# Reordering the first GEMM half, splitting a pair of PSUM banks into two tiles, and spreading the last stores

## The chip, the cores and the metric

The kernel runs on one core of a Trainium2 chip. The metric is the device time of one execution in microseconds (us). The engines are PE (TensorE), DVE (VectorE), ACT (ScalarE), POOL (GpSimd) and SP (SyncE), which here only issues DMAs. Each engine runs its own instructions in the order in which they were written to its queue.

## The reference, cut to what matters

Eight batches of 576 tokens go through Nystrom attention (8 heads of 64, 32 landmarks) and two feed-forward stages. The weights `w_in` and `w_out` are 64-bit floats, all else is 32-bit.

```python
q_lm = q.reshape(B, H, 32, 18, D).mean(axis=3); k_lm = ...   # landmarks: means of 18 rows
A, Bm, C = sm(q, k_lm), sm(q_lm, k_lm), sm(q_lm, k)          # three softmaxes
for _ in range(6): Z = 2 * Z - Z @ Bm @ Z                    # inverse of Bm by iteration
x = A @ Z @ C @ v                                            # B*S x 512
r = np.maximum(x @ w_in, 0); x = (r * r) @ w_out             # first stage, d_ff 2048
e = argmax(x @ w_gate)                                       # second stage: one of 8 experts per token
out = gate * sigmoid(x @ w_output_gate)[e] * (relu(x @ w1[e]) @ w2[e])
```

## The kernel before, in words

**Stages.** The prologue computes batch 0's attention and begins to convert the weights. Then `gemm(b)` runs the first feed-forward stage for one batch after the other, in two halves of tokens (`c`, 288 columns each) and 16 tiles of the hidden dimension (`f`); "tile" below means one such step. At last `experts` runs the second stage, for each batch with the expert most of its tokens chose; tokens with another expert would be done in a loop at the end (`others`). The attention of batch b+1 is cut into steps (`unit`), which are issued between the matmuls of `gemm(b)`.

**A tile.** Six matmuls of `hp` (the hidden tile, one PSUM bank in `self.hps`), then ACT makes `r` (relu), `gh` (r squared, rounded), and `g`, r squared in full: on DVE in the first half of batch 0 (line 1273), on ACT in all others (line 1275). DVE makes `gl = g - gh` (line 1276). Two tiles later `second` multiplies `gh` and `gl` with the tile's rows of `w_out` into four accumulators (12 matmuls). Products are made of high and low parts, each in a fast 32-bit form.

**The first half's other work.** In the first half of batch 0 the weights are still being converted from 64 bits (`convert`). For each piece of 128 x 512 a 512 KB transfer brings `raw`; one cast on POOL or ACT makes `m`, one on ACT makes `r` (`r<-raw`), and DVE joins them to a `w` or `wf` (`bits`). `convert_on(f)` issues `CONV` = 2 such steps behind each tile's relu. `split_out` turns each tile's `w` into `hi` (ACT) and `lo` (DVE). `first_g_of` (tiles 1, 4, 7) folds batch 0's values into `w_in` (`chunk`, the matmuls into `two` or banks; `split_g`). `SUMS_AT` places the sums of batch 1's queries, which DVE reduces for batches 0 and 1 and POOL for the others.

**What sets the order.** The program issues instructions in the order of this text, but a scheduler in the tile framework orders each engine's queue by a simulated timeline and by priority; `high_priority(URGENT)` marks the tile's products. `follow(a, b)` makes a stand behind b in that order without a semaphore: an instruction of another engine does not wait for it on the chip. `point()` stands behind each tile's relu and three times in each `second`; it adds `self.rate` to a sum, and for each whole unit issues one step of the side work. `RATES` gives the rate for a batch and half, and until tile `B1_FROM` the sum is held down. `behind(mm)` makes a tile's first product stand behind the side step of `PACE` = 20 steps ago. `hold`, `release` and `held` put off stores and loads while weights are converted. When the conversion ends (half 1, tile 0), `swap` opens new pools and loads.

**Batch 1's steps** (`unit`): six transposes of keys, with the second sums of queries in the fourth; landmarks of keys, landmarks of queries (`bank<-ident,sums` on PE), scores C, softmax B, values, seven steps of the inverse (`dg`, `eu`, `wz` on DVE between products on PE), the transpose of `wz` that gives the weights for `chunk`, and the softmax of A. From batch 2 on keys and queries are flipped by DVE transposes instead (`flipped`, lines 576 and 580), with POOL copies.

**Tiles of a pair of banks.** `products`, `chunk` and the experts' fifth accumulator take `self.pair`, one tile of two PSUM banks:

```python
two = self.pair.tile([128, 2, 512], F32, tag="p", name="two")
banks = [two[:, 0], two[:, 1]]
```

**The last stores.** The last batch's five output tiles are stored in 18 DMAs of 64 KB by a table, `("ssss", "pppp", "sspp", "aaas", "ss")`, one letter a store: s for SP, p for POOL, a for ACT. The fifth tile is made first, then the others; ACT evacuates the second and fourth, DVE the first and third.

Of the kernel before, what the change touches and what calls it, by code (L numbers as in the profile page):

```python
# [23 lines left out]
LM = 32  # L24
# [17 lines left out]


CONV = 2.0
SUMS_AT = {7: ("q", 0)}
OUT_AHEAD = 3
FIRST_G = (1, 4, 7)
B1_FROM = 3

URGENT = 2000  # L50
G_FIRST = 2

RATES = {(0, 0): 0.3, (0, 1): 0.8}
RATE = 0.4

PACE = 20
# [13 lines left out]
STEP = 1  # L70
# [51 lines left out]
class Kernel:  # L122
    def __init__(self, tc, ins, out):
        self.tc, self.nc, self.out = tc, Lanes(self, tc.nc), out
        self.lanes, self.strict, self.due_conv, self.loaded, self.late_loads, self.at_half, self.last_hp = {}, None, 0.0, 0, 0, (0, 0), None
        self.q, self.k, self.v, self.w_in, self.w_out, self.w_gate, self.w_og, self.w1, self.w2 = ins
        self.conv, self.last_pe, self.last_h, self.marks = None, None, None, []
        self.lead = False
        self.large, self.fence, self.fenced = [], None, 0
        self.now, self.later, self.side, self.rate, self.due = 0, [], iter(()), 0.0, 0.0  # L130
        self.gt, self.at, self.made, self.g_done, self.last_gb = {}, {}, {}, 0, None
        self.held, self.whole, self.raws, self.pacer, self.ahead, self.early = [], {}, {}, None, None, None
        self.wf, self.wo, self.qk, self.vt, self.wts, self.wis = {}, {}, {}, {}, {}, {}
# [49 lines left out]
    def convert(self, jobs):  # L183
# [29 lines left out]
        def scale(i):  # L213

            raw, m = st[i], tops[i % CONV_BUFS]
            r = pool.tile([128, W], I32, tag="cr", name="r", bufs=CONV_BUFS)
            top = m.bitcast(F16).rearrange("p (n t) -> p n t", t=2)[:, :, 1]
            high = raw.bitcast(BF16).rearrange("p (n t) -> p n t", t=4)[:, :, 2]
            ops = []
            low = raw.rearrange("p (n t) -> p n t", t=2)[:, :, 0].bitcast(U32)  # L220
            if self.last_h is None and i > 4 and i % 2:
                ops.append(nc.scalar.activation(out=top, in_=high, func=ACTF.Copy))
            else:
                ops.append(nc.gpsimd.tensor_copy(out=top, in_=high))
            if self.last_h is None:
                ops.append(nc.scalar.activation(out=r, in_=low, func=ACTF.Copy, scale=2.0 ** -13))
            else:
                ops.append(nc.scalar.activation(out=r, in_=low, func=ACTF.Copy, scale=0.5, bias=2.0 ** 11))
                wide.add(i)
            if self.last_h is not None:  # L230
                for op in ops:
                    self.follow(op, self.last_h)
            st[i] = m, r

        def bits(i):
# [249 lines left out]
    def bank(self):  # L485
        b = self.banks.pop(0)
        self.banks.append(b)
        return b.tile([128, 512], F32, tag="b", name="bank")

    def load_next(self, pool=None):  # L490

        if self.conv is not None and self.loaded >= 8:
            self.late_loads += 1
            return
        self.loaded += 1
        key = next(self.order, None)
        if key is None:
            return
        nm, b, hg = key
        t = self.qk[key] = (pool or self.ld).tile([128, SEG, D], F32, tag="qk", name="t", bufs=1 if pool else 3)  # L500
        src = (self.k if nm == "k" else self.q)[b, 4 * hg:4 * hg + 4]
        self.paced(self.nc.sync.dma_start(
            out=t.rearrange("p s d -> p (s d)"), in_=src.rearrange("h (l s) d -> (h l) (s d)", s=SEG)
        ))
# [16 lines left out]
    def sums(self, u, nm, hg):  # L521

        if nm + "s" not in u:
            u[nm + "s"] = self.sm.tile([128, 2, 2, D], F32, tag=f"{nm}s", name="sums", bufs=1)
        s, t = u[nm + "s"][:, hg], self.qk[nm, u["b"], hg]
        if not u["pe"]:
            t = t.rearrange("p s d -> p (s d)")
            x = self.sm.tile([128, SEG // 2 * D], F32, tag="st", name="st", bufs=1)
# [39 lines left out]
    def flipped(self, u, nm, hg):  # L568
# [4 lines left out]
        def put(to, p, i):  # L573
            src = t[p, :, LM * i:LM * i + LM]
            if nm == "k":
                self.nc.vector.transpose(  # L576
                    out=to.rearrange("p (r i l) -> p i r l", r=R6, l=LM), in_=src.rearrange("p (i r) d -> p i r d", r=R6)
                )
            else:
                self.nc.vector.transpose(out=to.rearrange("p (s l) -> p s l", l=LM), in_=src)  # L580


        for i in range(2):
# [43 lines left out]
    def products(self, u, nm, lm, i):  # L627

        if u["early"] and i:
            banks = [self.bank() for _ in range(2)]  # L630
        else:
            two = self.pair.tile([128, 2, 512], F32, tag="p", name="two")
            banks = [two[:, 0], two[:, 1]]
        with self.run_of():
            for half in (1, 0):
                for j in range(4):
# [172 lines left out]
    def values(self, u, hg):  # L809
# [15 lines left out]
        )  # L825
        if (b, 1) not in self.vt:
            self.load_v(b, 1)
        elif hg == 1:
            self.hold(lambda: self.load_v(b + 1, 0))

    def inverse(self, u, i):

# [131 lines left out]
    def unit(self, u):  # L964

        both = [(hg, i) for hg in range(2) for i in range(3)]
        if u["pe"]:
            for hg, i in both:
                self.transposed(u, "k", hg, i)
                if (hg, i) == (1, 0):  # L970
                    self.sums(u, "q", 1)
                yield STEP
        else:
            for hg in range(2):
# [9 lines left out]

        self.landmarks(u, "k")
        yield STEP
        self.landmarks(u, "q")
        yield STEP

# [51 lines left out]
    def prologue(self, right):  # L1041
# [66 lines left out]
        next(pw, None)  # L1108
        cv(2)
        self.release(2)  # L1110
        self.load_next()
        self.values(u, 0)
        for _ in range(3):
            next(a0)
# [24 lines left out]
    def chunk(self, b, n, rows):  # L1139

        if b == 0 and n == 0:
            banks = [self.bank() for _ in range(2)]
        else:
            two = self.pair.tile([128, 2, 512], F32, tag="p", name="two")
            banks = [two[:, 0], two[:, 1]]
        with self.run_of():
            for g in (1, 0):
                for j in (3, 2, 1, 0):
# [72 lines left out]
    def convert_on(self, f):  # L1221

        self.due_conv += CONV
        while self.due_conv >= 1.0:
            self.due_conv -= 1.0
            next(self.conv, None)
        self.release(1)
        if f in SUMS_AT:
            self.sums(self.ahead, *SUMS_AT[f])

# [5 lines left out]
    def gemm(self, b, swap=None, last=None):  # L1236

        nc = self.nc
        for c in range(2):
# [6 lines left out]
            for f in range(NFC):  # L1246
# [20 lines left out]
                gh = self.g3.tile([128, HC], F32R, tag="gh", name="gh", bufs=3)  # L1267
                gl = self.g3.tile([128, HC], F32R, tag="gl", name="gl", bufs=3)
                with self.tc.high_priority(URGENT):
                    nc.scalar.activation(out=r, in_=hp[:, 0:HC], func=ACTF.Relu)  # L1270
                    nc.scalar.activation(out=gh, in_=r, func=ACTF.Square)  # L1271
                    if (b, c) == (0, 0):
                        nc.vector.tensor_tensor(out=g2, in0=r, in1=r, op=ALU.mult)
                    else:
                        nc.scalar.activation(out=g2, in_=r, func=ACTF.Square)  # L1275
# [9 lines left out]
                if c == 1 and f == 0 and self.conv is not None:  # L1285
# [4 lines left out]
                    self.release(len(self.held))  # L1290
                    for _ in range(self.late_loads):
                        self.load_next()
                    swap()
                if c == 0 and f == 8:
                    self.load_at(b, 1)
                if last is not None and c == 1 and f in (5, 8, 11, 13):
                    next(last)
# [136 lines left out]
    def jobs(self):  # L1434
# [3 lines left out]
        def job(b):  # L1438
            def store(t, y):
# [3 lines left out]
                    return  # L1443

                q = dict(s=nc.sync, a=nc.scalar, p=nc.gpsimd)
                for i, e in enumerate(("ssss", "pppp", "sspp", "aaas", "ss")[t][:rows_of(t) // LM]):
                    q[e].dma_start(out=rows[4 * t + i], in_=y[LM * i:LM * i + LM])

            return dict(
# [8 lines left out]
    def experts(self, jobs):  # L1458
# [66 lines left out]
        def second(i, h, acc):  # L1525
# [2 lines left out]
            first, last = f == 0, f == NF2 - 1  # L1528
            if first:
                acc.extend(self.acc.tile([128, DM], F32, tag="b", name="y") for _ in range(4))  # L1530
                acc.append(self.pair.tile([128, 2, 512], F32, tag="p", name="y")[:, 0])
            ends = []

            def in_turn(mm, begin, end):
# [236 lines left out]
```

## Time and profile before

| | |
|---|---|
| runs | 1245.49, 1246.2, 1247.0 us; median 1246.2 |
| profiled execution | 1246.25 us; span from first to last instruction 1244.2 us |
| busy share of the span | PE 97%, ACT 49%, DVE 49%, POOL 31% |
| mean granted TensorE clock | 0.984 |
| PE's busy tenths in 40 slices | 6889899899999999999999999999999999999996 |
| DVE's | 7893755766556555655646532234332323323231 |
| granted clock in the slices | 8699999999999999999999999999999999999999 |
| DMA engines' | 9963043152232142142042210153434435443231 |

A slice is 31.1 us; a digit is the busy share in tenths (9 is 90% or more; the clock's are tenths of full speed). The prologue takes the first slice, the first half of batch 0 ends at about 101 us, its second half at about 157; the GEMMs take until about 800 us, the experts the rest.

### The profile page before, as it was taken

The page shows a single profiled execution, that of the slowest core. Times are in us where ns is not written, and L with a number is a line of the kernel's source. Part 1 is how long each engine was busy: PE and PEld are TensorE (multiplying, and loading weights), DVE is VectorE, ACT ScalarE, POOL GpSimd, SP SyncE. Part 2 cuts the span into 40 slices and gives each one's busy share as a digit, 9 for nine tenths or more (in the row PEclk, how much of TensorE's full clock was granted, in tenths as well). Part 3 has the DMA queues.
Part 4 walks back from the last instruction along what each step waited for, and adds up shares of the span by engine and source line. Part 5 has one row for each costly group of instructions (what it writes and reads, how often), then busy time and mean ns, then how long its engine had stood idle before and what let it go on. Part 6 is the DMA issues. An engine that isn't in the chain of part 4 may idle for free.

```text
span 1244.2 us, 25082 instructions
## 1 busy us (share of the span) xinstructions
PE 1207.0 (97%) x9838; PEld 1078.3 (87%) x9838; DVE 606.4 (49%) x1512; ACT 610.0 (49%) x1413; POOL 390.0 (31%) x524
## 2 busy tenths in 40 slices
PE   6889899999999999999999999999999999999996
PEld 4679788989989989989989989998888888888885
DVE  7893755766556555655646532234332323323231
ACT  6675355555564564555565555543342433434331
POOL 6540440613332241340341100253342433424220
PEclk8699999999999999999999999999999999999999
DMA  9963043152232142142042210153434435443231
GB/s 341 365 240 107 20 160 120 31 174 77 72 142 78 66 148 77 56 158 78 25 169 59 95 63 1 40 169 87 136 115 138 139 92 160 116 130 111 82 97 40
DMA packets 88407, 142.24 MB, mean 114 GB/s; under 512 B 6430, under 2 KB 61758, under 8 KB 84702
## 3 DMA queue, kind: packets, MB, share of 16 engines
q1 hardware_dynamic: 87854, 139.97, 34.6%
q8 instruction: 79, 1.29, 0.4%
q0 software_dynamic: 288, 0.43, 0.1%
q14 instruction: 42, 0.34, 0.1%
q10 hardware_dynamic: 144, 0.20, 0.1%
HBM read 117.47 MB, written 23.11 MB: 113 GB/s over the span
## 4 chain that ended last, share of the span: by engine, by line
PE 91%; DVE 5%; DMA 1%; ACT 1%; issue 1%; POOL 0%; POOLq 0%; ACTq 0%; DVEq 0%; SPq 0%
PE hp L475 32%; PE acc L475 31%; PE y L475 17%; PE two L471 4%; PE bank L471 2%; PE bank L104 2%; PE bank L483 1%; DVE x L576 1%; PE acc L104 1%; PE pl L471 1%; DMA raw<-in_moe_w_in_dram 1%; DMA raw<-in_moe_w_out_dram 0%; PE hp L104 0%; DVE lo L104 0%; DVE ma L687 0%
## 5 line engine op out<-in xcount | busy, mean ns | idle before, releaser
L475 PE MATMUL acc<-gl,hi 128*128 128x288 f32 x964 | 273.2, 301 | 2.7 <-DVE gl L104 1.6
L475 PE MATMUL acc<-gh,lo 128*128 128x288 f32 x964 | 270.0, 297 | 0.0
L475 PE MATMUL hp<-ab,gb 128*128 128x288 f32 x1434 | 239.3, 302 | 0.1
L475 PE MATMUL y<-s,h 128*128 128x512 f32 (+1 forms) x896 | 223.3, 396 | 0.8 <-ACT h L1516 0.5
L1276 DVE TENSOR_TENSOR gl<-g,gh 128x288 fp32r<-128x288 f32 x224 | 115.0, 514 | 214.6 <-ACT g L1275 212.2
L475 PEld LDWEIGHTS hp<-xs,s 128*128 128x128 f32 x1536 | 212.4, 188 | 7.2 <-DVE ls L1727 0.3
L475 PEld LDWEIGHTS hp<-ab,gb 128*128 128x128 f32 x1434 | 202.4, 189 | 18.7 <-issue 12.7
L475 PE MATMUL hp<-xs,s 128*128 128x288 f32 x1536 | 217.0, 295 | 0.2 <-DVE ls L1727 0.2
L1270 ACT ACTIVATE r<-hp 128x288 f32<-128x288 f32 x224 | 92.0, 411 | 229.5 <-PE hp L475 228.3
L475 PE MATMUL acc<-gh,hi 128*128 128x288 f32 x964 | 198.8, 301 | 0.1
L475 PEld LDWEIGHTS y<-s,h 128*128 128x128 f32 (+1 forms) x896 | 160.7, 184 | 38.2 <-ACT h L1516 0.7
L475 PEld LDWEIGHTS acc<-gl,hi 128*128 128x128 f32 x964 | 181.9, 189 | 9.5 <-issue 2.2
L475 PEld LDWEIGHTS acc<-gh,lo 128*128 128x128 f32 x964 | 182.0, 189 | 1.4 <-issue 1.4
L280 POOL TENSOR_TENSOR s<-r,s 128x256 fp32r<-128x256 f32 x128 | 102.0, 818 | 234.0 <-ACT s L268 234.0
L475 PEld LDWEIGHTS acc<-gh,hi 128*128 128x128 f32 x964 | 149.6, 188 | 19.8 <-ACT gh L1271 14.2
L1516 ACT ACTIVATE h<-hp 128x288 fp32r<-128x288 f32 x128 | 52.5, 411 | 188.0 <-PE hp L475 172.5
L1519 DVE SCALAR_TENSOR_TENSOR h<-hp,h 128x64 fp32r<-128x64 f32 (+2 forms) x192 | 62.6, 354 | 167.0 <-ACT h L1516 166.5
L268 ACT CAST s<-r 128x512 fp32r<-128x512 f32 x128 | 77.6, 617 | 70.7 <-PE y L475 56.9
L1271 ACT ACTIVATE gh<-r 128x288 fp32r<-128x288 f32 x224 | 99.5, 444 | 6.4
L274 DVE TENSOR_TENSOR s<-r,s 128x512 fp32r<-128x512 f32 x64 | 50.6, 791 | 102.8 <-ACT s L268 102.8
L1275 ACT ACTIVATE g<-r 128x288 f32<-128x288 f32 x224 | 96.0, 428 | 0.0
L587 POOL COPY x<-x 32x576 f32<-32x576 f32 x48 | 32.9, 685 | 173.4 <-DVE x L576 106.0
(263 smaller groups left out, 1327.9 us busy)
## 6 DMA issues: line engine op xcount, KB each, us to landing
r<-in_moe_w_dram SPq DMA_DIRECT2D x128, 256.0 KB
wi<-win SPq DMA_DIRECT2D x28, 1024.0 KB
t<-in_k_dram SPq DMA_DIRECT2D x16, 576.0 KB
t<-in_q_dram SPq DMA_DIRECT2D x16, 576.0 KB
v<-in_v_dram SPq DMA_DIRECT2D x32, 288.0 KB
x_d<-x SPq DMA_DIRECT2D x16, 576.0 KB
xr<-x_d SPq DMA_DIRECT2D x16, 576.0 KB
raw<-in_moe_w_in_dram SPq DMA_DIRECT2D x16, 511.8 KB
```

The costliest lines, as they stand in the source:

```text
L104: return self.kernel.in_lane(self.name, fn(*args, **kw))
L268: hi = self.nc.scalar.copy(out=t[:, 0], in_=raw)
L274: lo_eng.tensor_tensor(out=t[:, 1], in0=raw, in1=t[:, 0].bitcast(F32), op=ALU.subtract)
L280: self.nc.gpsimd.tensor_tensor(out=out[:, p], in0=in0[:, p], in1=in1[:, p], op=op)
L471: self.in_run(lambda: self.nc.tensor.matmul(out, **kw))
L475: mm = self.nc.tensor.matmul(out, **kw)
L1270: nc.scalar.activation(out=r, in_=hp[:, 0:HC], func=ACTF.Relu)
L1271: nc.scalar.activation(out=gh, in_=r, func=ACTF.Square)
L1275: nc.scalar.activation(out=g2, in_=r, func=ACTF.Square)
L1276: nc.vector.tensor_tensor(out=gl, in0=g2, in1=gh.bitcast(F32), op=ALU.subtract)
L1516: nc.scalar.activation(out=h[:, t0:t1], in_=hp[:, 0:HC], func=ACTF.Relu)
L1519: nc.vector.scalar_tensor_tensor(out=h[:, to + a:to + z], in0=hp[:, a - t0:z - t0], scalar=0.0, in1=h[:, a:z].bitcast(F32), op0=ALU.max, o ...
```

## The change

- First half: batch 1's query sums move from tile 7 and the fourth side step to tiles 10 and 11, with a wait in the steps before the queries' landmarks; the side steps begin at tile 5 instead of 3, with a rate of 0.9 instead of 0.8 in the second half. The third load of batch 1's queries and keys (its first query tile) is issued at tile 2 instead of in the prologue, its first values after `swap` instead of held in the prologue. A conversion's second cast is ordered behind the newest relu instead of behind its product. For odd tiles g is made on ACT. The second half's operand is made at tile 13 instead of 8 (batch 0 alone).
- Batch 2's key and query flips on DVE are ordered behind the newest tile's first product.
- The pair of banks is two tiles of one bank each.
- The last stores have another table.

```diff
-SUMS_AT = {7: ("q", 0)}
+SUMS_AT = {10: ("q", 0), 11: ("q", 1)}
-B1_FROM = 3
+B1_FROM = 5
-RATES = {(0, 0): 0.3, (0, 1): 0.8}
+RATES = {(0, 0): 0.3, (0, 1): 0.9}
@@ scale, in convert
-            if self.last_h is not None:
-                for op in ops:
-                    self.follow(op, self.last_h)
+            if self.last_relu is not None:
+                for op, e in zip(ops, (self.last_h, self.last_relu)):
+                    self.follow(op, e)
+    def two(self):
+        return [self.pair.tile([128, 512], F32, tag=f"p{i}", name="two") for i in range(2)]
@@ sums
+        u[nm + "n"] = hg + 1
@@ put, in flipped
-                self.nc.vector.transpose(
+                op = self.nc.vector.transpose(
...
+            if u["b"] == PE_BATCHES:
+                self.follow(op, self.last_h)
@@ products; chunk alike
-            two = self.pair.tile([128, 2, 512], F32, tag="p", name="two")
-            banks = [two[:, 0], two[:, 1]]
+            banks = self.two()
@@ values
-        elif hg == 1:
-            self.hold(lambda: self.load_v(b + 1, 0))
+        elif hg == 1 and self.conv is None:
+            self.load_v(b + 1, 0)
@@ unit
                 self.transposed(u, "k", hg, i)
-                if (hg, i) == (1, 0):
-                    self.sums(u, "q", 1)
...
         self.landmarks(u, "k")
         yield STEP
+        while u.get("qn", 0) < 2:
+            yield STEP
         self.landmarks(u, "q")
@@ prologue
         self.release(2)
-        self.load_next()
@@ convert_on
         self.release(1)
+        if f == 2:
+            self.load_next()
@@ gemm
-                    nc.scalar.activation(out=r, in_=hp[:, 0:HC], func=ACTF.Relu)
+                    self.last_relu = nc.scalar.activation(out=r, in_=hp[:, 0:HC], func=ACTF.Relu)
...
-                    if (b, c) == (0, 0):
+                    if (b, c) == (0, 0) and f % 2 == 0:
...
                     for _ in range(self.late_loads):
                         self.load_next()
+                    self.load_v(1, 0)
                     swap()
-                if c == 0 and f == 8:
+                if c == 0 and f == (8 if b else 13):
                     self.load_at(b, 1)
@@ store, in jobs
-                for i, e in enumerate(("ssss", "pppp", "sspp", "aaas", "ss")[t][:rows_of(t) // LM]):
+                for i, e in enumerate(("spsp", "apsp", "sapp", "saps", "sa")[t][:rows_of(t) // LM]):
@@ second, in experts
-                acc.append(self.pair.tile([128, 2, 512], F32, tag="p", name="y")[:, 0])
+                acc.append(self.pair.tile([128, 512], F32, tag="p0", name="y"))
```

## Rows read from the trace of the kernel before

**Rows 1.** Stretches: length, busy us (instructions) by engine, clock, DMA share, GB/s.
```profile
36.00:48.00 12.00, 8.14 (x41) 4.55 (x34) 8.71 (x13) 7.21 (x14) 6.84 (x8) 0.50 1.04 372
62.00:76.00 14.00, 10.65 (x88) 9.30 (x86) 14.00 (x19) 10.89 (x25) 7.96 (x9) 1.00 0.81 315
76.00:101.20 25.20, 25.20 (x243) 22.98 (x228) 21.10 (x55) 16.66 (x40) 5.66 (x5) 1.00 0.44 160
132.40:157.40 25.00, 20.55 (x154) 17.76 (x146) 18.52 (x46) 8.89 (x22) 13.68 (x21) 0.93 0.00 1
157.40:200.00 42.60, 42.56 (x420) 36.46 (x420) 29.20 (x77) 25.89 (x66) 14.55 (x23) 1.00 0.40 138
200.00:1233.90 1033.90, 1031.60 (x8033) 928.71 (x8033) 465.76 (x1180) 489.48 (x1138) 304.29 (x406) 1.00 0.31 98
1233.90:1244.20 10.30, 0.00 (x0) 0.00 (x0) 0.03 (x1) 0.67 (x1) 2.55 (x6) 0.70 0.41 112
```
**Rows 2.** Waits of PE from 36 to 76: total us, times, longest.
```profile
PE acc L104 <- DVE gl L104: 2.4, 3, 1.1
PE hp L104 <- ACT r L104: 2.0, 2, 1.8
PE two L104 <- DVE wf L104: 1.5, 1, 1.5
```
**Rows 3.** Timeline of ACT: start, us, instruction, idle before it, releaser.
```profile
42.13 0.66 ACT L104 ACTIVATE r<-raw 128x512 int32<-128x512 uint32 x1 [2.79 <-DMA raw<-in_moe_w_in_dram]
...
43.73 0.40 ACT L104 ACTIVATE r<-hp 128x288 f32<-128x288 f32 x1
...
1233.88 0.69 ACT L1582 ACTIVATE yo<-y,rt 128x512 f32<-128x512 f32 x1 [0.72 <-PE y L475]
```
**Rows 4.** Timeline of PE around tile 1's product.
```profile
40.40 1.96 PE L104 MATMUL two<-wf,wt 64*32 64x512 f32 x16
44.18 1.81 PE L104 MATMUL hp<-ab,gb 128*128 128x288 f32 x6 [1.82 <-ACT r L104]
```
**Rows 5.** The chain that ended last: start, us, what.
```profile
34.40 7.63 DMA raw<-in_moe_w_in_dram
```
**Rows 6.** Timeline of SP, which issues the loads.
```profile
33.01 0.33 SPq L104 DMA_DIRECT2D t<-in_q_dram  x1
```
**Rows 7.** Groups on DVE, 0 to 160: count, busy us, mean ns, idle before.
```profile
L104 DVE TENSOR_REDUCE sums<-t 128x32 f32<-128x576 f32 x12 | 13.3, 1175 | 0.2 <-DMA t<-in_k_dram 0.2
L104 DVE TENSOR_TENSOR g<-r 128x288 f32<-128x288 f32 x16 | 7.7, 480 | 1.8 <-ACT r L104 1.8
...
L576 DVE STREAM_TRANSPOSE x<-t 32x576 f32<-32x576 f32 x4 | 3.1, 769 | 0.1
L576 DVE STREAM_TRANSPOSE x<-t 128x576 f32<-128x576 f32 x4 | 2.9, 754 | 0.0
```
**Rows 8.** Timeline of PE late in the second half.
```profile
138.05 0.40 PE L475 MATMUL acc<-gl,hi 128*128 128x288 f32 x1 [1.61 <-DVE gl L104]
```
**Rows 9.** Timeline of PE: batch 1's landmarks, its last transpose, the next product.
```profile
84.49 0.66 PE L104 MATMUL bank<-ident,sums 128*64 128x128 f32 x8
...
151.89 0.30 PE L483 MATMUL bank<-ident,wz 128*128 128x128 f32 x1 [0.43 <-DVE wz L849]
...
156.30 1.09 PE L471 MATMUL two<-wi,wt 64*32 64x512 f32 x16
```
**Rows 10.** Timeline of DVE in the second batch's GEMM.
```profile
189.61 2.76 DVE L580 STREAM_TRANSPOSE x<-t 128x576 f32<-128x576 f32 x4 [0.48 <-PE two L471]
```
**Rows 11.** The last stores by issuer: count, ns min/median/max, first and last start.
```profile
L1447 SPq DMA_DIRECT2D out_dram<-yo x9: 314/419/1532, 1232.6 to 1237.8; - x9
L1447 POOL DMA_DIRECT2D out_dram<-yo x6: 496/498/547, 1233.5 to 1236.0; - x6
L1447 ACTq DMA_DIRECT2D out_dram<-yo x3: 386/448/1883, 1234.6 to 1236.9; - x3
```
**Rows 12.** Waits of ACT over the whole span.
```profile
ACT gb L1190 <- DVE gb L1191: 16.5, 20, 1.4
```

More of the change, by code (lines that the diff above doesn't have):

```diff
@@ L124, in __init__ @@
         self.tc, self.nc, self.out = tc, Lanes(self, tc.nc), out
-        self.lanes, self.strict, self.due_conv, self.loaded, self.late_loads, self.at_half, self.last_hp = {}, None, 0.0, 0, 0, (0, 0), None
+        self.lanes, self.strict, self.due_conv, self.loaded, self.late_loads, self.at_half, self.last_hp, self.last_relu = {}, None, 0.0, 0, 0, (0, 0), None, None
         self.q, self.k, self.v, self.w_in, self.w_out, self.w_gate, self.w_og, self.w1, self.w2 = ins
@@ L579, in put @@
             else:
-                self.nc.vector.transpose(out=to.rearrange("p (s l) -> p s l", l=LM), in_=src)
+                op = self.nc.vector.transpose(out=to.rearrange("p (s l) -> p s l", l=LM), in_=src)
+            if u["b"] == PE_BATCHES:
+                self.follow(op, self.last_h)
         for i in range(2):
@@ L1143, in chunk @@
         else:
-            two = self.pair.tile([128, 2, 512], F32, tag="p", name="two")
-            banks = [two[:, 0], two[:, 1]]
+            banks = self.two()
         with self.run_of():
```

## The prediction

> **What bounds the kernel now.** The page's first and second parts (in the table above) say that TensorE is the engine to watch: 97% busy, nearly all slices at 9. So I cut the span into stages and asked for each engine's busy time in each [rows 1]; the reader looks for stages where PE's busy time falls short of the stage. From 200.0 to the last matmul at 1233.9 PE is busy 1031.6 of 1033.9 us: an edit that shortens nothing on PE can win 2.3 us there at most, over 1000 us. What is left to win lies in four places: 36 to 48 us (idle 3.9 us, at half clock), 62 to 76 us (idle 3.35), 132.4 to 157.4 us (idle 4.45, mean granted clock 0.93) and the 10.3 us after the last matmul.
>
> In the first two places the waits of PE between 36 and 76 us [rows 2] name the causes: 2.4 us for VectorE's gl, 2.0 for ScalarE's r, 1.5 for VectorE's wf, 5.9 us together (what is left of the idle time lies before tile 0's product). Two readings explain them. On ScalarE the relu of tile 0 starts at 43.73 only, though PE had gone on to other work at 40.40: ahead of it in ScalarE's order stood a conversion cast, r<-raw, that waited 2.79 us for its transfer [rows 3, 4]. PE's next product then waited 1.82 us for that relu [rows 4]. From 62 to 76 us VectorE is busy 14.0 of 14.0 us [rows 1]: everything that PE waits for stands in VectorE's queue. The third place is the same picture: PE waits 1.61 us for a gl in it [rows 8], and among VectorE's groups there the two largest are eight transposes at line 576, 3.1 + 2.9 us, which flip batch 2's keys, work that nobody needs before the next GEMM [rows 7].
>
> **The change part by part.**
>
> *Casts behind the relu (last_relu).* The two casts of tile 0's conversion steps are now ordered after tile 0's relu, so the relu can start at about 40.5 instead of 43.73. PE's 1.82 us goes; next late is gl of tile 0, which comes forward with the relu. Bounds: 0 (the cast now waits behind the relu and its conversion is later) to 2.5 us (with tile 0's share of the gl waits). Taken: 1.8. The same transfer is shortened, too: it was issued at 34.40 and landed 7.63 us later [rows 5], right behind a 576 KB load of batch 1's queries at 33.01 [rows 6], which moves to tile 2; at the 372 GB/s of that stretch [rows 1] the load is 1.6 us of transfer. The load of batch 1's values, two DMAs of 288 KB, leaves the stretch altogether. Neither is a second gain: they secure the first. Both now stand later in SP's queue; the values stand behind batch 2's key loads there, and the side step that reads them waits if they are late (in the last rival).
>
> *Queries' sums to tiles 10 and 11, and g of odd tiles on ScalarE.* Four reductions of 1.175 us, 4.7 us, leave the full stretch from 62 to 76, and with them the products g of tiles 5, 7 and 9, 3 x 0.48 = 1.4 us [rows 7]; ScalarE, busy 10.9 of 14.0 there, takes the latter. 6.1 us of VectorE's 14.0 against 3.35 us of idle PE: these waits can go whole. But the reductions come back in tiles 10 and 11. From 76 to 101.2 us VectorE is busy 21.1 of 25.2 [rows 1]: 4.1 us free, 5.5 with the odd tiles' g gone, for 4.7. The first half of that stretch is the fuller one, so I let a third of the 4.7 (1.6 us) be met by PE again. For waits of 5.9 us in all, the two edits together give 5.9 - 1.6 = 4.3 us; bounds 0 and 5.9, and below nothing if all 4.7 of the reductions stood ahead of the landmarks that PE runs next (5.9 - 4.7 still leaves 1.2, so a loss needs more than them).
>
> *Second batch's steps from tile 5, at 0.9 a point in the second half.* The steps' matmuls are the same; they move from a stretch in which PE waited to one in which it is full, for two transposes of keys, about 0.5 us, inside the margin above. The wait for both sums stops the side steps only (one step is lost, at tile 10). What it costs if the chain that follows becomes late is the last rival.
>
> *Batch 2's transposes behind the product of their own GEMM (flipped).* Eight transposes, 6.0 us, leave the 25.0 us in which VectorE is busy 18.5 [rows 1, 7]. The idle 4.45 us and the lowered clock, 25.0 x 0.07 = 1.7 us of PE's work, make 6.2 us that can go. What is late next is batch 1's own chain of inverses, PE to VectorE and back, for which I leave 2.0 us. Taken: 4.2; bounds 1.5 and 6.2. They come to the stretch from 157.4 to 200, where VectorE is busy 29.2 of 42.6. The same eight transposes of batch 2's queries already lie there, four of them in one piece at 189.61 [rows 10], and PE is idle 0.04 us in all of it [rows 1]. Taken: 0; bound 2 us.
>
> *Pair of banks as two tiles.* With one tile ScalarE's second cast waited for VectorE's read of the other bank, 16.5 us in 20 waits [rows 12]. No wait of PE hangs on them in the full stages: 0, bounds -0.5 and +0.2. `load_at` at tile 13, the second half's operand: ScalarE and GpSimd work with two tiles left to hide it: 0.
>
> *Last stores.* Before, SP issues 9 of the 18 stores, from 1232.6 to 1237.8, GpSimd 6, ScalarE 3 [rows 11]; from SP's last issue to the span's end are 6.4 us, which stay. After, SP has 7, GpSimd 7, ScalarE 4. GpSimd: 7 x 0.50 from about 1233.2 ends near 1236.7. ScalarE now issues stores between its evacuations, 0.39 to 0.45 each; two before the last evacuation, 1233.88 [rows 3], so that this starts some 0.6 us later, ends near 1235.2, and SP's last issue starts near 1236.1, or 1.1 later if the slow issue there (1.53 against 0.42) repeats. A gain of 0.6 to 1.7; taken 1.2, bounds 0.4 and 2.0.
> The Trainium skill ("DMA: Bandwidth & Descriptors", "Rules for kernel authors") speaks against such a split: stores spread over several issuers share the same DMA engines, and only issue time is saved. By it alone the gain would be the lower bound, 0.4 us; the DMA share of 0.41 after the last matmul [rows 1] says that issue is what bounds, and 1.2 stays.
>
> **The sum.** 4.3 + 4.2 + 1.2 = 9.7 us less. The profiled execution took 1246.25 us (span 1244.2 and 2.05 around it), which is the median of the runs (1246.2) within 0.1: 1246.25 - 9.7 = 1236.5 us. With all lower bounds of the gains and all bounds of loss (2 from 157.4 on, 0.2 for the pair) it is 1246.6, with all upper bounds 1231.6.
> The Trainium skill ("TensorE: Matmul & The Clock Gate", "What's actually happening") says the clock is halved after idleness and given back once PE has been kept busy. The trace agrees (0.50 from 36 to 48 us with PE idle a third of it); by the rule an earlier end of the waits would also bring full speed earlier, and the sum would be about 1 us better.
>
> **The rivals.**
> *Only the second half gains.* VectorE is the limit from 62 to 90 us by its total work: what leaves tiles 7 to 9 is met in tiles 10 and 11, where the landmarks stand on PE right behind the sums. For it: VectorE is full there, and the sums are read at once. Against: 5.5 us free for 4.7. Then 1246.25 - 4.2 - 1.2 = 1240.9.
> *Only the first half gains.* The stall from 132.4 is batch 1's chain, not batch 2's transposes. For it: its steps hang one on another through PE and VectorE, whatever else VectorE does. Against: the 6.0 of 18.5 us that VectorE is rid of. Then 1246.25 - 4.3 - 1.2 = 1240.8.
> *It doesn't do what it says.* The orders of the engines come from a simulated timeline; the hoisted casts and transposes may be replaced by others of the same length. Then about 1245.
> *Slower: batch 1's chain sets the end of the second half.* From the landmarks of its queries at 84.49 to its last transpose at 151.89 it takes 67.7 us, and the next batch's product stands at 156.30 [rows 9]. The change begins it two tiles later: a tile of the first half is (101.2 - 44.18) / 15 = 3.8 us (tile 1's product [rows 4] to the second half's start, the bound of a stretch in [rows 1]), so 7.6. If the chain keeps its length, it ends at 159.8, 3.5 us past the product, PE stands idle and the clock falls for another 1.7: 1246.25 + 5.2 - 1.2 = 1250.3. What the first half gains brings the chain's start forward by as much, so it is slower only if that gain is under about 1.5 us. For it: dependent steps, and the values' load now late in SP's queue. Against: the rate of 0.9, and that the chain was long because VectorE was full.
>
> **Chances.** The forecast 0.57, second half only 0.15, first half only 0.12, no effect 0.07, slower 0.09. The time is the forecast's, 1236.5 us (its own range 1232 to 1240). The range is 1231 to 1244.5: it takes in both half gains, and leaves out the slow rival, most of no effect and a few hundredths below. A change of under 0.2%, 2.5 us, can't be told from none here: faster 0.83, same 0.08, slower 0.09.
>
> **What would show it.** Tile 0's relu on ScalarE within 0.5 us of its product; no wait of PE for gl or wf from 60 to 76 us; no line 576 before the second GEMM; PE idle under 2.5 us and the clock at 1.00 around 130 to 155 us; SP's last store issued 0.6 to 1.7 us earlier against the last matmul. Wrong would be PE waiting for `sums` at tiles 10 to 12, or for `eu` and `wz` at the end of the second half as now, or for batch 2's transposes after 157 us.

## The result, and the profile after

The changed kernel takes 1260.64 us (median; 1260.09 to 1262.17) beside 1246.6 us of the kernel before (1245.49 to 1247.59): ratio 1.0115, 95% interval 1.0097 to 1.0132, so 14 us slower. The forecast was 1236.5 us.

The profiled execution took 1261.19 us, its span is 1259.4 us. To see where the time came, I cut both traces where the first relu of a half batch starts, so that a stretch holds the same work in both. The windows of the kernel before (columns as in [rows 1]):

```profile
102.16:161.59 59.43, 54.98 (x509) 49.72 (x511) 29.48 (x70) 26.36 (x65) 15.16 (x22) 0.97 0.21 68
161.59:306.46 144.87, 144.80 (x1421) 127.62 (x1420) 91.10 (x237) 81.45 (x206) 46.17 (x72) 1.00 0.35 113
306.46:450.19 143.73, 143.42 (x1281) 129.17 (x1282) 82.91 (x206) 78.90 (x196) 51.73 (x79) 1.00 0.30 101
450.19:815.54 365.35, 364.53 (x3258) 333.91 (x3257) 184.02 (x502) 200.90 (x503) 81.78 (x124) 1.00 0.23 76
815.54:1233.90 418.36, 417.22 (x2466) 370.44 (x2464) 134.17 (x309) 152.03 (x296) 139.16 (x155) 1.00 0.39 114
```

The same stretches of the changed kernel, ahead of them the one that answers to the first of [rows 1], behind them the one that answers to the last:

```profile
36.00:48.00 12.00, 9.49 (x62) 5.07 (x47) 11.16 (x17) 9.62 (x20) 7.79 (x9) 0.71 1.04 341
...
98.71:158.11 59.40, 56.64 (x511) 51.40 (x509) 24.77 (x64) 27.50 (x67) 10.64 (x15) 0.94 0.21 68
158.11:316.88 158.77, 155.58 (x1424) 129.79 (x1424) 97.53 (x249) 81.22 (x207) 53.89 (x84) 1.00 0.32 104
316.88:461.57 144.69, 144.69 (x1281) 129.21 (x1280) 80.65 (x201) 77.83 (x195) 49.00 (x75) 1.00 0.29 100
461.57:832.16 370.59, 369.78 (x3258) 334.91 (x3257) 182.78 (x501) 199.24 (x503) 82.30 (x124) 1.00 0.23 75
832.16:1250.46 418.30, 417.21 (x2466) 370.45 (x2464) 134.10 (x309) 152.01 (x295) 138.55 (x155) 1.00 0.38 115
1250.46:1259.40 8.94, 0.02 (x1) 0.00 (x0) 0.11 (x1) 0.69 (x1) 3.11 (x7) 0.74 0.46 129
```

Difference of the lengths, in us: the first half, up to 102.16 and 98.71, -3.45; the second half of batch 0, -0.03; batch 1 and the first half of batch 2, +13.90; the next three halves, +0.96; batch 4 to the last relu, +5.24; the expert part, -0.06; the tail, -1.36. Together +15.2, the difference of the spans. So the first half and the stores gained about what was forecast, the second half nothing, and 20 us came in places where the forecast had put 0. In batch 1 and the first half of batch 2 some of it is waiting: PE is idle 3.2 us there (158.77 less 155.58), 0.07 before, most of it for VectorE's gl (changed kernel, PE, 158 to 320):

```profile
PE acc L475 <- DVE gl L1281: 2.7, 4, 1.5
```

From batch 4 on waiting is not the cause. TensorE runs the same 3258 matmuls, was full before and is full after, yet its busy time grows by 5.25 us (364.53 to 369.78). A wait doesn't show like that. The groups of PE show it; of the kernel before (columns: engine, tiles, shape, count | busy us, mean ns of one | idle before):

```profile
PE 1207.0 (97%) x9838; PEld 1078.3 (87%) x9838; DVE 606.4 (49%) x1512; ACT 610.0 (49%) x1413; POOL 390.0 (31%) x524
L475 PE MATMUL acc<-gl,hi 128*128 128x288 f32 x964 | 273.2, 301 | 2.7 <-DVE gl L104 1.6 <-DVE gl L1276 1.1
L475 PE MATMUL hp<-ab,gb 128*128 128x288 f32 x1434 | 239.3, 302 | 0.1
L471 PE MATMUL two<-wi,wt 64*32 64x512 f32 x448 | 30.5, 601 | 0.0
L471 PE MATMUL two<-x,lm 64*32 64x288 f32 x416 | 22.6, 415 | 0.0
```

and of the changed kernel:

```profile
PE 1221.6 (97%) x9838; PEld 1079.0 (86%) x9838; DVE 604.4 (48%) x1504; ACT 608.7 (48%) x1421; POOL 387.8 (31%) x525
L475 PE MATMUL hp<-ab,gb 128*128 128x288 f32 x1434 | 242.2, 303 | 0.7 <-ACT r L104 0.5
L471 PE MATMUL two<-wi,wt 64*32 64x512 f32 x448 | 34.6, 601 | 0.0
L471 PE MATMUL two<-x,lm 64*32 64x288 f32 x416 | 31.9, 415 | 0.0
```

PE's busy time grew by 14.6 us with the same 9838 matmuls. The two groups that write `two`, the pair of banks, hold 13.4 of it (9.3 and 4.1), at an unchanged mean of one matmul, 415 and 601 ns. A mean that stays while the group's busy time grows says that fewer of them run at the same time. The timeline of PE shows it. Batch 5's product run of the kernel before (start, us, instruction), 8 matmuls in 16 records (two records of the trace for each of these matmuls):

```profile
465.92 0.68 PE L471 MATMUL two<-x,lm 64*32 64x288 f32 x4
466.52 0.40 PE L475 MATMUL acc<-gl,hi 128*128 128x288 f32 x1
...
471.50 0.26 PE L1411 MATMUL pc<-x,ones 128*32 128x40 f32 x2
471.69 0.70 PE L471 MATMUL two<-x,lm 64*32 64x288 f32 x12
472.32 0.40 PE L475 MATMUL acc<-gl,hi 128*128 128x288 f32 x1
```

The same run in the changed kernel:

```profile
476.47 0.69 PE L471 MATMUL two<-x,lm 64*32 64x288 f32 x8
477.09 0.35 PE L471 MATMUL pt<-lg,i 128*32 128x80 f32 x8
...
478.88 0.67 PE L471 MATMUL two<-x,lm 64*32 64x288 f32 x2
479.48 0.40 PE L475 MATMUL acc<-gl,hi 128*128 128x288 f32 x1
...
481.27 0.67 PE L471 MATMUL two<-x,lm 64*32 64x288 f32 x2
481.87 1.07 PE L475 MATMUL hp<-ab,gb 128*128 128x288 f32 x6
...
484.46 0.68 PE L471 MATMUL two<-x,lm 64*32 64x288 f32 x4
485.07 0.40 PE L475 MATMUL acc<-gl,hi 128*128 128x288 f32 x1
```

From its start to the start of what follows, a piece of 2 records holds PE for 0.60 us, of 4 for 0.60 or 0.61, of 8 for 0.62, of 12 for 0.63. A piece costs by being a piece, not by its length, and it also costs beside it: behind a piece the first large matmul holds PE 0.24 us and the next ones 0.13 (changed kernel, starts at 479.48, 479.72 and 479.85), and the hp group grew by 2.9 us. Counting as one piece what runs of one such group with nothing else between on PE, there are 67 pieces of `two` in the trace before and 85 after. Why the run fell apart stands on VectorE, whose transposes make the operand x (changed kernel):

```profile
477.97 0.77 DVE L584 STREAM_TRANSPOSE x<-t 32x576 f32<-32x576 f32 x1
...
479.75 0.77 DVE L584 STREAM_TRANSPOSE x<-t 32x576 f32<-32x576 f32 x1
```

They end at 478.74 and 480.52, and the two pieces of 2 records start at 478.88 and 481.27: some matmuls of a run have their operand earlier than others. The program issues a run bank by bank, four matmuls each, and two of the four have their operand late. While both banks were one tile, the matmuls behind a late one stayed behind it: 4 records went ahead, and the run was cut once. With two tiles 8 go ahead, and large matmuls get in between the others. That these 8 are the early ones of both banks is read from the code and the counts; the rows don't name the bank. The Trainium skill ("TensorEngine Tiling (Array Packing)", "Tiling Modes") says that a change of tiling mode drains TensorE; it gives no price. The trace fits that, though it doesn't show a drain by itself: a 64*32 piece between 128*128 matmuls holds PE 0.60 us however short it is.

### The profile page after: what moved, and what is told of

Read it like the earlier page. It is cut to its first block, busy times and chain, and to the rows that moved or that the text cites. A ratio compares the mean times of both kernels' runs of the same rounds, so it can differ in the third digit from the quotient of the medians.

```text
span 1259.4 us, 25031 instructions
## 1 busy us (share of the span) xinstructions
PE 1221.6 (97%) x9838; PEld 1079.0 (86%) x9838; DVE 604.4 (48%) x1504; ACT 608.7 (48%) x1421; POOL 387.8 (31%) x525
## 4 chain that ended last, share of the span: by engine, by line
PE 88%; DVE 6%; DMA 4%; ACT 1%; issue 1%; POOL 0%; SPq 0%; POOLq 0%; DVEq 0%; ACTq 0%
PE hp L475 31%; PE acc L475 30%; PE y L475 17%; PE two L471 5%; PE bank L471 3%; DMA win<-wf 1%; PE bank L483 1%; DMA v<-in_v_dram 1%; DVE x L580 1%; DMA raw<-in_moe_w_in_dram 1%; PE pl L471 1%; DMA raw<-in_moe_w_out_dram 1%; DVE w L104 0%; DVE gl L1281 0%; DVE ma L692 0%
## 5 line engine op out<-in xcount | busy, mean ns | idle before, releaser
L475 PE MATMUL hp<-ab,gb 128*128 128x288 f32 x1434 | 242.2, 303 | 0.7 <-ACT r L104 0.5
```

Source lines behind the costliest of these rows:

```text
L475: mm = self.nc.tensor.matmul(out, **kw)
```

## The experiments

Theory: the cut runs cost the time, and they come from the two tiles. Rivals: the new order of batches 0 to 2 costs it; or two tiles cost by themselves. The 14 runs below, each in five rounds beside the kernel before (1246.0 to 1246.7 us in the four groups). Pieces are those of the traces; the expectations count them in the programs as built, which lists some cuts that the trace doesn't show:

| kernel | us | ratio to before, interval | pieces |
|---|---|---|---|
| before | 1246.2 | 1 | 67 |
| changed | 1260.64 | 1.0115 (1.0097, 1.0132) | 85 |
| changed, one tile (e1) | 1244.02 | 0.9984 (0.9975, 0.9993) | 69 |
| two tiles alone (e2) | 1260.69 | 1.0113 (1.0097, 1.0128) | 86 |
| moved flips alone (e3) | 1247.00 | 1.0003 (0.9994, 1.0012) | 69 |
| stores alone (e4) | 1245.30 | 0.9990 (0.9981, 0.9999) | 67 |
| changed, runs in order (e5) | 1250.35 | 1.0034 (1.0021, 1.0048) | 78 |
| changed, one tile, flips back (e6) | 1243.13 | 0.9977 (0.9966, 0.9988) | 67 |
| whole runs alone (e8) | 1246.20 | 0.9999 (0.9990, 1.0008) | 61 |
| e6 with whole runs (e9) | 1244.45 | 0.9982 (0.9973, 0.9991) | 61 |
| changed, whole runs (e10) | 1244.28 | 0.9988 (0.9980, 0.9997) | 67 |
| casts, odd g, loads, stores (e11) | 1241.40 | 0.9964 (0.9951, 0.9977) | 71 |
| e11 and moved flips (e12) | 1241.48 | 0.9962 (0.9949, 0.9975) | 73 |
| casts alone (e13) | 1242.65 | 0.9975 (0.9966, 0.9983) | 67 |
| two tiles and whole runs (e14) | 1249.87 | 1.0028 (1.0018, 1.0038) | 67 |
| e11, two tiles, whole runs (e15) | 1241.06 | 0.9956 (0.9943, 0.9969) | 66 |

**Which part costs the time: e1 and e2.** e1 is the changed kernel with

```diff
-        return [self.pair.tile([128, 512], F32, tag=f"p{i}", name="two") for i in range(2)]
+        two = self.pair.tile([128, 2, 512], F32, tag="p", name="two")
+        return [two[:, 0], two[:, 1]]
```

and e2 the kernel before with the opposite edit.

> The changed kernel with the pair of banks back as one tile [128, 2, 512]; all else as changed. Theory (broken runs): a run of small matmuls that is cut costs a whole pass more for each piece, 0.69 + 0.68 us for two pieces against 0.72 us for the whole run of x,lm, so about 0.65 us a piece, and the traces have 67 such pieces before and 85 after. With one tile the program has 74 of them: 11 x 0.65 = 7 us, up to 11 x 0.75 = 8 us with what DVE's later results add, come back, so 1252 to 1254 us if that is all, and less (down to 1246.6: 1246.6 + 7 x 0.65 - 3.45 of the first half - 1.4 of the stores) if each cut run also holds up the engine behind it. Rival (the new order in the first two batches sets the loss, the pair is innocent): 1258 us or more.

> The kernel before with only the pair of banks as two tiles. The program has 86 pieces of small matmuls against 67 of the kernel before. Theory (broken runs): 19 x 0.65 = 12.4 us more, so 1259 us (1256 to 1261), with the busy time of TensorE 12 to 15 us up. Rival (the loss is the order of the first two batches): 1246.6 us, within 1 us.

One tile takes 16.6 us off the changed kernel, and two tiles alone make the kernel before as slow as the whole change did, as expected of e2. The rival of the new order is out; the cost of the pair is 14.5 us. e1 came out below its expectation, whose lowest bound was 1246.6: its gain is larger than the pieces alone (16 x 0.65 = 10.4). Part of the rest is the time beside a piece; how much that is worth was not tried.

**Two tiles or cut runs: e5 and e10.** e5 adds to the changed kernel, for each matmul of a run, an order behind the one before it; e10 only lets the product runs begin with the matmul whose operand comes last:

```diff
+        prev = self.last_pe                        (e5, in_run)
...
+        self.follow(self.last_pe, prev)
```

```diff
-                for j in range(4):                 (e10, products)
+                for j in (2, 3, 0, 1):
```

> The changed kernel, its pair still two tiles, with each small matmul of a run put behind the one before it on TensorE's order (no semaphore: an order only). Theory (broken runs): what costs time is the pieces, not the two tiles; the program has 74 pieces, as many as with one tile, so the time is that of the changed kernel with one tile, 1244.0 us (1243 to 1247). Rival (two banks in two tiles cost by themselves, in their waits or in where the tiles lie): 1258 to 1261 us.

> The changed kernel as it is, its pair two tiles, with the product runs begun with the matmul whose operand comes last (order 2, 3, 0, 1 of j). The program has 73 pieces of small matmuls against 85 in the changed kernel's trace; what is left broken are chunks' and products' runs of the first batches, cut between the two banks. Theory (price by the piece, 0.6 us for x,lm and 1.0 us for wi,wt): 12 x 0.6 = 7.2 us less than the changed kernel's 1260.6, 1253.4 us, and up to 3 us of it given back where the kernel before gave back 3.1 us for the same edit (its run starts later, and VectorE's softmax comes in one lump): 1253 to 1257 us. Rival (two tiles cost by themselves): 1259 us or more.

Both keep two tiles. With 78 pieces the time is 1250.35, with 67 it is 1244.28 us: most of the loss goes with the pieces, and two tiles need not cost by themselves. Neither met its expectation. e5 should have taken 1243 to 1247 us; 78 pieces are left in its trace, where e1 has 69, and the count is not all: from batch 4 on it has the 27 pieces of the kernel before and still takes 366.83 us against 365.35. Of e10 I had expected less, 1253 to 1257; it has 18 pieces less than the changed kernel, not 12 as counted ahead, and its batches from 4 on are faster than those of the kernel before. The run of above is one piece now, held 0.65 us (e10, PE; then the same stretches as above, and the two groups):

```profile
472.88 0.72 PE L471 MATMUL two<-x,lm 64*32 64x288 f32 x16
473.53 0.26 PE L1417 MATMUL pc<-x,ones 128*32 128x40 f32 x2
```

```profile
154.29:308.33 154.04, 151.70 (x1425) 129.33 (x1425) 95.50 (x248) 80.94 (x206) 52.48 (x83) 1.00 0.32 107
308.33:451.15 142.82, 142.47 (x1277) 128.70 (x1278) 80.45 (x202) 77.78 (x196) 49.81 (x77) 1.00 0.29 101
451.15:814.24 363.09, 362.56 (x3258) 333.32 (x3257) 180.76 (x501) 200.08 (x503) 82.44 (x124) 1.00 0.23 77
```

```profile
L471 PE MATMUL two<-wi,wt 64*32 64x512 f32 x448 | 34.6, 601 | 0.0
L471 PE MATMUL two<-x,lm 64*32 64x288 f32 x416 | 19.9, 415 | 0.0
```

From batch 4 on e10 takes 363.09 us, 7.5 less than the changed kernel and 2.3 less than the kernel before, with 12 pieces there against 21 and 15: 0.83 and 0.75 us a piece. What it still loses lies in batch 1 and the first half of batch 2, 154.04 against 144.87 us, where runs of wi,wt are still cut between the banks (34.6 against 30.5 us) and the moved flips lie.

**Is a piece always worth its 0.6 us: e8 and e9.** The edit of e10 alone, in the kernel before (e8) and in e6 (e9).

> The kernel before with one edit: the eight matmuls of a product run begin with the one whose operand comes last (order 2, 3, 0, 1 of j for 0, 1, 2, 3), so that the first of them waits and the other seven follow at once. The program has 61 pieces, one a run, against 67. Theory (broken runs): 6 x 0.65 us = 3.9 us less, 1242.3 us (1241.5 to 1243.5). Rival (the pieces' own time is covered, and what two tiles cost is something else): 1246.2 us, within 1 us; slower if the later start of a run delays VectorE's softmax.

> The changed kernel with one tile for the pair, the flip transposes where they were before, and the product runs begun with the matmul whose operand comes last. By the theory the sum of the two: 1241.2 us less 3.9 us = 1237.3 us (1236 to 1239). By the rivals 1241 us (only the first half) or 1244 to 1245 us (neither).

No. In e8 the group falls by 4.0 us, as it should, and the time stays, as the rival said. The same view of e8:

```profile
L475 PE MATMUL acc<-gl,hi 128*128 128x288 f32 x964 | 275.3, 303 | 4.2 <-DVE gl L1276 2.8 <-DVE gl L104 0.9
...
L471 PE MATMUL two<-x,lm 64*32 64x288 f32 x416 | 18.6, 415 | 0.0
```

PE's matmuls on gl are busy longer there than in the kernel before (273.2) and wait 4.2 us for VectorE, against 2.7. With one tile the whole run starts when the last operand comes, and VectorE then gets both banks at once; gl waits behind them. That VectorE's batch is the reason is read from these rows and was not tried by itself. From batch 4 on PE is idle 2.97 us of 367.39 in e8, against 0.82 before. e9 says the same: 1237.3 us was expected, it took 1244.45, no faster than e6 (1243.13), with 367.46 us from batch 4 on. With two tiles (e10, the same edit) the batches from 4 on kept the gain.

**The moved flips: e3, e6, e12.** e3 is the kernel before with

```diff
+            if u["b"] == PE_BATCHES:
+                self.follow(op, self.last_h)
```

> The kernel before with only the flip transposes of the third batch (index 2) put behind the last gate tile's work. The prediction's step: 4.2 us less, 1242.4 us. Theory of the trace after: the second half gains nothing, because the second batch's own softmax and inverse fill VectorE there, and the transposes cost up to 2.4 us where they lie now, so 1246.6 to 1249 us; and if the 74 pieces of small matmuls that the program has (67 before) cost 0.65 us each as well, 7 x 0.65 = 4.6 us more, 1251 us (1249 to 1254).

> The changed kernel with one tile for the pair and with the third batch's (index 2) flip transposes left where they were before. The traces so far: with the moved transposes alone the second half of batch 0 is 5.0 us shorter, and 4.5 us of it are gone by batch 4 (index), 2.0 us as idle time of TensorE behind gl and the rest as busy time; with all but the two tiles 4.5 us are won by the end of batch 0 and all are gone by batch 4. Theory (the moved transposes give the loss back): without them the first half's 3.5 to 3.9 us stay, with the stores' 1.2 us that makes 1241.2 us (1240 to 1242.5). Rival (the batches 1 to 3 end at a time that something else sets, VectorE or a load, and eat whatever was won): 1244 to 1245 us.

The windows of e3 at the same work:

```profile
103.50:157.96 54.46, 52.91 (x509) 48.07 (x510) 24.20 (x64) 26.58 (x65) 10.97 (x15) 1.00 0.23 75
157.96:207.29 49.33, 47.95 (x460) 41.47 (x461) 30.62 (x81) 28.77 (x74) 17.58 (x29) 1.00 0.37 125
207.29:306.01 98.72, 98.72 (x973) 87.72 (x972) 62.34 (x162) 52.39 (x133) 31.90 (x49) 1.00 0.31 104
306.01:451.12 145.11, 144.08 (x1273) 128.14 (x1272) 86.29 (x207) 78.63 (x195) 53.20 (x82) 1.00 0.28 100
```

The second half falls from 59.43 to 54.46 us with the clock at 1.00: 5.0 won. Then 3.2 and 1.4 us are given back (148.05 against 144.87, 145.11 against 143.73), 0.4 is left, less than the 1.3 us by which the first half of this execution was longer (103.50 against 102.16), and the run ends no faster. One wait shows in the first of these stretches, where the flips lie now (e3, PE, 157 to 210):

```profile
PE acc L475 <- DVE gl L1278: 1.3, 1, 1.3
```

Beside it two runs are cut that were whole. e6, without the flips, is no slower than e1, but doesn't reach the expected 1241.2: its second half is 62.0 us long, 2.6 more than before, with one long wait (PE, 98 to 161):

```profile
PE bank L471 <- DVE dg L947: 4.2, 1, 4.2
```

That is batch 1's own chain, which the change starts two tiles later.

**The first half: e11, e12, e13.** e11 is e6 with the queries' sums, the rate and the start of batch 1's steps put back as here, e12 the same with the moved flips, e13 the kernel before with the casts' order alone:

```diff
-SUMS_AT = {10: ("q", 0), 11: ("q", 1)}
+SUMS_AT = {7: ("q", 0)}
-B1_FROM = 5
+B1_FROM = 3
-RATES = {(0, 0): 0.3, (0, 1): 0.9}
+RATES = {(0, 0): 0.3, (0, 1): 0.8}
...
+                if (hg, i) == (1, 0):
+                    self.sums(u, "q", 1)
```

> Of the change only the casts behind the relu, the odd gates' products, the moved loads and the new stores; the pair one tile, the flip transposes, the queries' sums, the rate and the tile from which the second batch's steps start as before. Theory (the moved sums make the second half longer: with them, and without the moved flips, 2.6 us of the first half's 3.7 us are lost again there, behind dg and at half the clock): the first half gains 2.5 to 3.5 us and keeps it, with the stores' 1.2 us that makes 1242 us (1241 to 1243.5). Rival (any earlier start of the second half is lost in it, whatever is moved): 1245 us.

> The same with the flip transposes of the third batch moved as well. From the runs so far: the first half gains 2.5 to 3.5 us, the second half 5.0 us more, batches 1 to 3 give back 4.5 us, the stores 1.2 us: 1241.5 us (1240.5 to 1243). Rival (batches 1 to 3 give back all that was won by their start, as with the changed kernel with one tile, where 4.5 us were won and 4.6 given back): 1245 us.

> The kernel before with one edit: the converter's casts on ScalarE put behind the last gate tile's relu instead of its first matmul. The prediction's step: 1.8 us less, 1244.2 us, won before the first relu at 43.7 us. Rival (the cast is only later by as much, and the weights that wait for it with it): 1246.0 us, within 0.5 us.

All three forecasts of direction held. In its trace e13 reaches the second half 3.2 us earlier and the last relu 4.4 us earlier (the trace is of its fastest execution, 1240.44 us; its runs go up to 1246.01), the others 3.0 and 2.5 us earlier at the second half: nearly all of the first half's gain is the casts. e11 is 1.7 us faster than e6, which the later sums and steps would cost, but the two intervals overlap; in the traces e11 ends batch 0 3.0 us earlier (157.40 against 160.44). e12's flips add nothing to e11.

**The stores: e4.** The kernel before with the changed table alone:

```diff
-("ssss", "pppp", "sspp", "aaas", "ss")
+("spsp", "apsp", "sapp", "saps", "sa")
```

> The kernel before with only the last stores' queues dealt out anew. The prediction's step: 1.2 us less (0.4 to 2.0); by the trace after, whose end lies 8.95 us behind the last matmul against 10.36 us, 1.4 us less: 1245.2 us. Rival (the stores' data transfer sets the end, whichever queue issues it): 1246.6 us, within 0.3 us.

The ratio says 1.2 us less, as the prediction's step did, but its interval goes from 0.1 to 2.4. From one trace to the next the tail varies, too: behind the last matmul it is 9.3 to 10.4 us in the six traces with the old table and 8.9 to 9.6 in the ten with the new one.

**What two tiles are worth with whole runs: e14, e15.** e14 is e2 with the order of e10; e15 is e11 with both.

> The kernel before with the pair of banks as two tiles and the product runs begun with the matmul whose operand comes last (order 2, 3, 0, 1 of j), nothing else. The program has 73 pieces of small matmuls (67 before, 86 with the two tiles alone at 1260.7 us): product runs whole but for six runs of each kind cut between the banks in the first batches. Theory (the cut runs are the whole cost): 1260.7 us less 14 to 16 us as in the changed kernel (1260.6 to 1244.3 us), so 1245 to 1247 us, with about 0.65 us a batch won in the batches from index 4 on and as much lost before. Rival (the order helps the changed kernel through its moved transposes): 1252 us or more.

> The kernel with the casts behind the relu, the odd gates' products, the moved loads and the new stores (1241.4 us), with the pair as two tiles and the product runs in the order 2, 3, 0, 1. If the two tiles and the order alone are worth between -1 and +1 us: 1240.5 to 1242.5 us. If batches 1 to 3 lose their cut runs (12 pieces, 0.6 and 1.0 us each, less what the whole product runs win): up to 1245 us. If the steady batches' 0.65 us each stays without that loss: 1238 us.

e14 missed its expectation by 3 us. From batch 4 on it wins the same 2.3 us as e10 (363.09 us, too), but it loses 5.8 us in batch 1 and the first half of batch 2 (150.63 against 144.87), where five runs are still cut between the banks, and 2.5 us in the first half, where PE waits 3.9 us for gl (44 to 105) against 2.4 [rows 2]; why it does so there was not tried, and up to 1.3 us of such a difference shows in the traces of e3, e4 and e8, too, which have one tile. e15 shows no such loss in the first half and is, with e11 and e12, the fastest: 1241.06 us, 5.6 less than the kernel before beside it. Between the three no difference can be told.

## Why the prediction was wrong

**The step that failed** is "*Pair of banks as two tiles*": "No wait of PE hangs on them in the full stages: 0, bounds -0.5 and +0.2." It measured +14.5 us (e2). The step asked only which waits the edit takes away. It didn't ask what one tile had been doing for the order of PE: it kept a run of small matmuls together. The row to see it was there: a run cut in two, 465.92 and 471.69, whose pieces of 4 and 12 records hold PE 0.60 and 0.63 us. None of the rivals had it either; the slower one named another mechanism, batch 1's chain. Without this step the forecast would still have been too good: the rest of the change takes 2.2 us off (e1), not 9.7.

**Casts**: 1.8 forecast, bounds 0 to 2.5; alone 3.6 us by the medians and 3.1 by the ratio (e13, interval 2.1 to 4.2). The mechanism was right and its size too small: the sum took PE's wait alone, and the full clock comes earlier, too (below). Relu and cast stand as the prediction said they would (changed kernel, ACT; before, the relu stood at 43.73 [rows 3]):

```profile
41.31 0.41 ACT L104 ACTIVATE r<-hp 128x288 f32<-128x288 f32 x1 [0.70 <-PE hp L104]
41.62 1.25 ACT L104 ACTIVATE r<-raw 128x512 int32<-128x512 uint32 x2
```

**Sums and odd g**: 2.5 forecast. The later sums and steps gain at most 0.9 in the first half (3.86 in e1 against 3.0 in e11, no more than single traces differ) and cost 1.7 us over the whole, if anything (e6 against e11). Odd g, with the moved loads, shows no gain there: e11, which has them, wins 3.0 us in the first half, the casts alone 3.2 (e13). The waits for r and wf (2.0 and 1.5 us) are gone, but those for gl did not go: 3.8 us from 36 to 76 in the changed kernel, against 2.4 [rows 2]:

```profile
PE acc L104 <- DVE gl L104: 3.8, 3, 1.4
```

So the term of 4.3 for the first half came out near its size, 3.45, for one of its two reasons and with a clock that the sum had left out: that the size fits is in part luck.

**Flips**: 4.2 forecast in the second half; alone they win 5.0 there (e3). Of that place the prediction named PE's wait for gl, 1.61 us; the one for eu, of batch 1's chain, is longer there (2.2 us, before, PE, 102 to 158), and in e3 it is 0.9. The step failed in the line behind it, "Taken: 0; bound 2 us" for where they go: 4.5 us. Within the change even the 5.0 didn't show, since batch 1's chain had been moved later: with the chain where it was the second half takes 54.45 us (e12), with the chain later 58.80 (e1) and 59.40 (the changed kernel). PE's waits in the second half of the changed kernel (98.71 to 158.11) are mostly for the chain's softmax, and the clock stands at 0.94:

```profile
PE bank L471 <- DVE ma L698: 1.9, 1, 1.9
```

This is the mechanism of the slower rival, but its price was a few us of gain not had, not a loss.

**Stores**: 1.2 forecast; the tail is 1.36 shorter in this pair of traces, and e4 agrees, with a wide interval. SP's last issue starts at 1252.4, 1.9 us behind the last matmul, where it was 3.9 [rows 11]:

```profile
L1453 SPq DMA_DIRECT2D out_dram<-yo x7: 335/427/816, 1249.2 to 1252.4; - x7
```

**The bonus for an earlier full clock** was put at about 1 us beside the sum. The earlier clock did come. From 36 to 48 us the mean granted clock went from 0.50 to 0.71, and from 48 to 62 us it stands at 1.00 where it was 0.80 (kernel before, then the changed one):

```profile
48.00:62.00 14.00, 14.00 (x96) 13.00 (x96) 11.95 (x22) 11.24 (x23) 6.69 (x7) 0.80 1.04 346
48.00:62.00 14.00, 11.52 (x90) 9.88 (x89) 12.69 (x20) 10.62 (x23) 6.72 (x8) 1.00 1.01 378
```

From 36 us on, in stretches of 2 us, the clock is at half until 52 us in the kernel before, until 44 in e13 and until 42 in the changed kernel, where PE was busy from 40 to 44 us without a gap; before, it waited 1.82 us there [rows 4]. PE is then idle more, 2.5 us from 48 to 62, so not all of it is won. The rule of the Trainium skill ("TensorE: Matmul & The Clock Gate", "What's actually happening"), that the clock is given back once PE has been kept busy, agrees with these rows. What the clock is worth by itself was not tried. In the second half it is lower than before, 0.94 against 0.97.

## What to carry to other kernels

A tile is also an order: splitting one frees its halves one by one and lets a scheduler put other work between instructions that were one run. Before such a split, look at whether a group's busy time is less than its count times its mean (here 416 x 415 ns = 173 us in 22.6 us of busy time): then being together is what it lives on, and the price of a cut is read from the shortest piece that stands alone. Letting a run begin with the instruction whose operand comes last keeps it whole; here that took back what the two tiles cost (all of it in e10, most of it in e14), but with one tile it won nothing (e8, e9).

## What the runs showed that was not expected

A 64*32 piece of 2, 4, 8 or 12 records holds TensorE for 0.60 to 0.63 us between large matmuls, a whole run of 16 for 0.65; for wi,wt the row of a whole run lasts 1.09 us and that of each half 1.06. And an edit that takes 4.0 us off a full TensorE (e8) gave nothing, since the time came back as waits for VectorE, partly inside the busy time of the matmuls that wait.
